# A new order of all engines' work in a Mamba-2 scan with a low-rank mixer, and V loaded in one transfer

## The chip, the core and the metric

The kernel runs on one core of a Trainium2 chip. Its engines work at the same time, each through its own list of instructions in a fixed order: TensorE (PE, matrix products; its weight loads are shown as PEld), VectorE (DVE), ScalarE (ACT), GpSimd (POOL) and SyncE (SP), whose queue issues all transfers here. They meet through semaphores: an instruction that waits holds up all that stand behind it on its engine. The metric is the device time of one execution in microseconds (us).

## The reference

Four batches, 8 heads, 768 positions. First a Mamba-2 scan in chunks of 32 positions with head width 32 and state width 16, then a mixer over positions of rank 32 and a two-layer network over the 256 channels:

```python
# scan, per chunk of 32
cum = np.cumsum(log_a, -1);  M = (C @ B.T) * exp(cum_i - cum_j) * causal
y = M @ x + (C @ state) * exp(cum)
state = exp(sum(log_a)) * state + sum_j B_j x_j exp(cum_end - cum_j)
# mixer, x is y as (batch, seq, 256)
h = (x.transpose(0, 2, 1) @ U) @ V
u = x + h.transpose(0, 2, 1)
out = u + np.maximum(u @ w_ch1, 0.0) @ w_ch2
```

x, a, B and C are 32-bit. U, V, w_ch1 and w_ch2 arrive as 64-bit numbers and are made 32-bit on the chip from their two words.

## The kernel before, in words

A batch of 768 positions is cut into three pairs of blocks of 128, so there are 12 pairs. The core does for each pair the scan, and for each batch the mixer (`project`, `mixed`, `added`) and then, in three blocks of 256 positions, the network. The order of everything is written out by hand in `PLANS`: strings of words, read by `follow` from left to right. A word calls one step, which emits its instructions, and each engine runs the instructions it gets in the order of the words. So two steps on different engines may overlap, and two on the same engine never change places.

The number behind a letter of the scan is the pair, counted from the first pair of batch 1: -3, -2 and -1 are batch 0, 0 to 2 are batch 1, and so on. The words that matter here:

- B and X load a pair's B, C (three transfers) and x (two). w0 to w8 load parts of the weights, L is a later pair's B and X together. Words B, X, w and L are held: their first transfer waits until the last DVE instruction emitted ahead of the word is done (`until`, `hold`).
- A and K make the decay factors from a (`decays`, `keep`). F puts that many filler products ahead of the next bank that is taken.
- P or Q multiplies B and C with decays (DVE; Q does a quarter or a half: 0 and 1 are B's two blocks, 2 is C). T or V turns the result on PE, and ACT or DVE copies it out. D or E multiplies B with the decay to the chunk's end (POOL in batch 0, DVE later).
- g makes C times B (PE, four banks), m and M mask its halves (two DVE instructions each), s makes the states' increments (PE), u carries the state on (DVE, then POOL or ACT).
- n and i add the two parts of y (PE), j is the second half of i and begins with a small copy on DVE that waits for the products before it when nothing else does. y copies the result (ACT), t or O turns it to rows per position and copies it (ACT, for O-1.1 DVE).
- c0 is the conversion of U and V, c1 and c2 of w0 and w1, c3 of w2, and so on. A c word is one of three steps: DVE and ACT, ACT, then DVE (`to_fp32`). v spreads V over the partitions (`spread`). R splits a weight into a near and a far part (`refine`): ACT first, the second R word with DVE.
- p, x, a are project, mixed and added of a mixer, S splits a block. The first number of these words is how many batches the mixer lies behind batch 1: 1 is batch 0, 0 is batch 1. U1.j.i is a quarter i of the hidden layer of block j of batch 0 in 32-bit products (`plain`). It needs `added` of its half of the positions: block 0 needs a1.0, block 1 needs both a1.0 and a1.1. For the other blocks f, e and h are its first products, second products and the two DVE steps behind them (`first`, `second`, `third`). d is a piece of the second layer (`down`).

The PSUM banks on which PE writes are 2 of tag w, 3 of x and 3 of z. A step that needs a bank waits until the readers of an older one are done.

V has 32 rows of 768 numbers. `Vq` holds it as 128 rows of 192: before, rows 32q to 32q+31 are its q-th quarter of columns. `spread` makes of it `V4`, in which each group of 32 partitions holds the rows of V with one half of its columns, by eight products with pieces of the identity.

Of the kernel before, what the change touches and what calls it, by code (L numbers as in the profile page):

```python
# [33 lines left out]

PLANS = {
    0: (
        'B0 X0 B1 X1 B2 X2 V0 U0 B3 '),
    1: (
        'w0 F5 A0 w1 Q-3.0 Q-3.1 B4 A1 w2 Q-3.2 F4 V-3.0.0 V-3.1.1 Q-2.2 B5 X3 Q-2.0 Q-2.1 K0 '
        'D-3 w3 w4 g-3 m-3 D-2 V-2.0.2 s-3 u-3 F2 V-2.1.2 M-3 Q-1.1 n-3 s-2 X4 Q-1.0 g-2 u-2 '  # L40
        'Q-1.2 V-1.0.2 m-2 M-2 w5 F1 V-1.1.3 i-3 c0 B6 c0 E-1.0 E-1.1 F1 s-1 u-1 c0 g-1 w6 w7 '
        'j-3 y-3 n-2 i-2 j-2 y-2 P0 c1 c1 m-1 M-1 T0 t-2 T0 n-1 c1 i-1 c2 c2 v0 j-1 y-1 P1 T1 '
        'O-3.0 T1 g0 c2 c3 m0 M0 O-1.1 p1 g1 D1 D0 s0 c3 X5 P2 m1 M1 x1 a1.0 u0 U1.0.0 T2 T2 '
        'a1.1 c5 U1.1.0 c3 s1 c4 c5 c5 n0 R0 i0 y0 c4 U1.0.1 U1.1.1 R1 w8 c4 X6 L4 P3 D2 c6 c6 '
        'R2 g2 c7 c7 U1.1.2 U1.1.3 t0 u1 T3 T3 U1.0.2 m2 M2 c7 i1 c6 n1 L5 L6 c8 c8 y1 c9 c9 '
        'U1.0.3 d1.0 c8 d1.1 n2 R5 s2 R4 c9 d1.0 d1.1 S1.2 u2 i2 P4 y2 R1 R0 T4 t1 d1.1 D4 R4 '
        'f1.2.1 R5 R3 f1.2.0 P5 T4 D3 R7 R3 R2 R7 d1.0 d1.0 e1.2.0 e1.2.1 h1.2.0 d1.1 h1.2.1 '
        'f1.2.2 f1.2.3 R6 t2 e1.2.2 g4 m4 M4 p0 h1.2.2 g3 m3 e1.2.3 M3 T5 d1.0 T5 R6 d1.2 L7 '
        'd1.2 x0 s3 a0.0 h1.2.3 d1.2 d1.2 S0.0 d1.2 d1.2 d1.2 d1.2 a0.1 u3 f0.0.1 f0.0.0 P6 P7 '
        'f0.0.2 d1.2 d1.2 d1.2 d1.2 e0.0.0 e0.0.1 e0.0.2 d1.2 d1.1 f0.0.3 n3 s4 i3 y3 h0.0.0 '  # L50
        'e0.0.3 T6 T6 h0.0.1 u4 h0.0.2 g5 m5 M5 h0.0.3 d0.0 d0.0 d0.0 d0.0 D5 d0.0 i4 D6 n4 S0.1 '
        'y4 s5 u5 d0.0 f0.1.3 d0.0 d0.0 i5 n5 y5 s6 u6 f0.1.2 f0.1.0 d0.0 d0.0 S0.2 e0.1.2 '
        'h0.1.2 L8 e0.1.0 f0.1.1 d0.0 d0.0 T7 e0.1.1 h0.1.1 f0.2.2 e0.1.3 f0.2.0 e0.2.2 h0.1.3 '
        'h0.2.2 f0.2.1 e0.2.0 h0.1.0 d0.1 d0.1 d0.1 h0.2.0 t5 f0.2.3 e0.2.1 P8 d0.1 d0.1 d0.1 '
        'e0.2.3 h0.2.3 h0.2.1 D7 d0.1 d0.2 d0.2 d0.1 d0.2 d0.2 t3 T7 d0.1 d0.1 d0.2 d0.1 d0.1 '
        'd0.0 T8 T8 D8 d0.2 d0.2 d0.2 t4 g7 m7 M7 p-1 g6 m6 M6 s7 d0.2 d0.2 d0.2 u7 d0.2 x-1 '
        'a-1.0 a-1.1 d0.1 d0.2 S-1.0 i6 n6 s8 y6 i7 S-1.1 n7 y7 u8 f-1.0.1 g8 m8 M8 f-1.0.0 '
        'f-1.0.2 f-1.0.3 e-1.0.0 e-1.0.1 h-1.0.0 h-1.0.1 f-1.1.1 S-1.2 f-1.1.0 f-1.1.2 e-1.0.2 '
        'h-1.0.2 e-1.0.3 t6 e-1.1.0 f-1.1.3 e-1.1.2 h-1.1.2 d-1.0 d-1.0 d-1.0 h-1.1.0 d-1.0 '
        'f-1.2.2 e-1.1.3 f-1.2.0 e-1.1.1 d-1.0 h-1.0.3 d-1.0 d-1.0 h-1.1.1 e-1.2.2 h-1.2.2 '  # L60
        'e-1.2.0 d-1.1 d-1.0 d-1.1 h-1.1.3 h-1.2.0 d-1.1 d-1.1 d-1.1 d-1.1 t7 d-1.1 d-1.1 i8 n8 '
        'd-1.1 d-1.1 d-1.1 y8 t8 p-2 d-1.1 x-2 a-2.0 S-2.0 d-1.0 f-1.2.3 f-1.2.1 d-1.0 d-1.0 '
        'd-1.0 e-1.2.3 e-1.2.1 h-1.2.3 f-2.0.0 a-2.1 d-1.2 h-1.2.1 f-2.0.1 d-1.2 d-1.2 d-1.2 '
        'S-2.1 d-1.2 e-2.0.0 h-2.0.0 d-1.2 d-1.2 f-2.0.3 f-2.0.2 S-2.2 d-1.2 f-2.1.2 e-2.0.1 '
        'h-2.0.1 e-2.0.2 e-2.0.3 h-2.0.2 d-1.2 d-1.2 e-2.1.2 d-1.2 d-1.2 f-2.1.3 f-2.1.0 h-2.1.2 '
        'f-2.1.1 f-2.2.2 e-2.1.0 e-2.1.1 d-2.0 d-2.0 d-2.0 d-2.0 e-2.2.2 h-2.0.3 d-2.0 d-2.0 '
        'f-2.2.0 e-2.1.3 d-2.0 d-2.0 f-2.2.3 d-2.2 f-2.2.1 h-2.1.0 h-2.1.3 e-2.2.3 d-2.0 d-2.1 '
        'd-2.1 d-2.1 d-1.1 h-2.1.1 e-2.2.0 d-2.1 h-2.2.3 d-2.1 d-2.1 d-2.1 h-2.2.0 d-2.1 e-2.2.1 '
        'h-2.2.1 d-2.0 d-1.2 d-2.0 d-2.0 d-2.2 d-2.1 h-2.2.2 d-2.1 d-2.1 d-2.1 d-2.0 d-2.2 d-1.0 '
        'd-2.2 d-2.2 d-2.2 d-2.1 d-2.2 d-2.2 d-2.2 d-2.2 d-2.2 d-2.2 d-2.2 '),  # L70
}


# [1 line left out]
def kernel(  # L75
# [43 lines left out]
    Q = 32  # L119
# [38 lines left out]
    class Kept:  # L158
# [6 lines left out]
        def __getattr__(self, name):  # L165
# [23 lines left out]
    def hold(load, until):  # L189

        tc.add_manual_dep(load.ins, until.ins.name, mybir.DependencyInfo(
            mybir.DependencyClass.Sync, mybir.DependencyReason.DATA))

    def begin(**kwargs):
        op = nc.sync.dma_start(**kwargs)  # L195
        if until:
            hold(op, until.pop())
# [24 lines left out]
    UV = const.tile([P, 2, NC * RK], FP32)  # L222
    U_sb = UV[:, 0].rearrange("p (c r) -> p c r", c=NC)
    Vq = UV[:, 1]
    V4 = const.tile([P, VS], FP32)
    w1 = [const.tile([P, NCB, DF], FP32R, name=f"w1{i}") for i in range(3)]
    w1all = const.tile([P, NQ, NCB, W], FP32, name="w1f")
    w1f = [w1all[:, c] for c in range(NQ)]
    w2 = [const.tile([P, NM, DM], FP32R, name=f"w2{i}") for i in range(3)]
    weights = []  # L230

    def words_of(dst):
        p, i, j = dst.shape
        t = raw.tile([P, 2 * WCOLS], INT32, tag="words", name="words", bufs=NWORDS)
        weights.append((dst, t[:p, :2 * i * j]))
        return t[:p, :2 * i * j]

    def each(parts, *index):
        return [part[index] for part in parts]

    def load_words(dst, src):

        p, i, j = dst.shape
        t = words_of(dst)
        begin(out=t.rearrange("p (i j) -> p i j", i=i), in_=src)

    U2, V2, w12, w22 = (w.bitcast(INT32) for w in (moe_U, moe_V, moe_w_ch1, moe_w_ch2))
    every = slice(None)
    quarter = WCOLS // NCB
    w13 = w12.rearrange("(c p) m -> p c m", p=P)  # L250
    own = {}

    def load_v():
        own["UV"] = words_of(UV)
        for q in range(4):
            begin(out=own["UV"][ts(q, Q), 2 * NC * RK:], in_=V2[:, ts(q, 2 * NC * RK)])

    def load_u():
        begin(out=own["UV"][:, :2 * NC * RK].rearrange("p (c r) -> p c r", c=NC),
                          in_=U2.rearrange("(c p) r -> p c r", p=P))  # L260

    def load_w(n):
        if n < 2:
            if n == 0:
                own["w"] = words_of(w1f[0])
                weights.pop()
            dst, t = w1f[0][:, :, ts(n, P)], own["w"][:, ts(n, 2 * NCB * P)]
            weights.append((dst, t))
            begin(out=t.rearrange("p (i j) -> p i j", i=NCB),
                  in_=w13[:, :, ts(n, 2 * P)])  # L270
        elif n <= NQ:
            load_words(w1f[n - 1], w13[:, :, ts(n - 1, 2 * quarter)])
        else:
            m = 2 * (n - NQ - 1)
            load_words(w2[0][:, m:m + 2], w22[m * P:(m + 2) * P].rearrange(
                "(m p) d -> p m d", p=P))

    def load(k):
        if k < NB * NPR:
            load_bc(k)  # L280
            load_x(k)

# [45 lines left out]
    for g in range(2):  # L328
# [3 lines left out]
        out=la.rearrange("p b c h -> p b h c"),  # L332
# [180 lines left out]
    def turn(*args):  # L513
        for _ in turning(*args):
            pass
# [414 lines left out]
    def spread():  # L930

        v = [bank(t, VS // 2) for t in "xz"]
        for q in range(4):
            for i in range(2):
                rows = ts(2 * (q % 2) + i, Q)
                nc.tensor.matmul(out=v[i][ts(q, Q)], lhsT=ident[rows, rows], rhs=Vq[rows],
                                 start=True, stop=True, skip_group_check=True)
        for i in range(2):
            nc.scalar.copy(out=V4[:, ts(i, VS // 2)], in_=v[i])

# [22 lines left out]
    def ytokens_of(k, v):  # L963
# [3 lines left out]
                 M=lambda k: mask(k, (2, 3)), u=update, i=lambda k: inter(k, 0), n=intra,  # L967
                 j=crossed, y=yout, t=ytokens, L=load, Q=lambda k, c: prep(k, c, 1),
                 E=lambda k, c: decayed(k, c, 1), O=ytokens_of,
                 V=lambda k, c, v: turn(k, c, 1, "wx"[v // 2], vector if v % 2 else None))  # L970
    whole = dict(c=convert, R=refined, A=lambda i: decays(every_batch, "w", [i]),
                 K=lambda n: keep(every_batch, "z"), F=fill,
                 v=lambda n: spread())
# [54 lines left out]
```

## Time and profile before

| what | value |
|---|---|
| median of 3 runs | 226.31 us (225.0 to 226.91) |
| profiled execution, its own time | 225.08 us |
| span from its first to its last instruction | 223.4 us |
| mean granted clock of TensorE | 0.977 of full speed |
| PE busy | 213.6 us (96%), 3374 products |
| DVE busy | 164.5 us (74%) |
| ACT busy | 129.0 us (58%) |
| POOL busy | 6.6 us (3%) |
| bytes moved | 14.61 MB, mean 65 GB/s |

In the page's second part the span is cut in 40 slices of about 5.6 us; each digit is a busy share in tenths, PEclk the clock that TensorE was granted in tenths of full speed. In the view by stretches a line gives the stretch, its length, then busy us and number of instructions of PE, PEld, DVE, ACT and POOL, then the granted clock, the share of the transfer engines and GB/s. In the order of time a line gives start, duration, engine, line of the source, operation, operands and count, and in brackets how long the engine had been idle and what released it. All DVE work is emitted on line 169, a helper, so it is told apart by its tiles.

### The profile page before, as it was taken

Reading aid. Unit: us, or ns where it says so; the run is one execution under the profiler, and the core shown is the slowest. Engines: PE = TensorE matmul, PEld = TensorE weight load, DVE = VectorE, ACT = ScalarE, POOL = GpSimd, SP = SyncE. Lnnn points to the kernel's source line nnn. Section 1 sums busy time; section 2 is a strip of 40 time slices with the busy share of each in tenths; the row PEclk is TensorE's granted clock in tenths of the full one; section 3 lists DMA queues with packets and bytes.
Section 4 is the critical chain, followed back from the end, with each engine's and each line's share of the span. In section 5 each row is a group of like instructions: output and inputs, shape, how many; then the busy total and the mean of one; then the engine's idle time right before and its main releaser. Section 6 shows DMA issues by size and latency. Waiting matters only on the chain.

```text
span 223.4 us, 7740 instructions
## 1 busy us (share of the span) xinstructions
PE 213.6 (96%) x3374; PEld 191.7 (86%) x3374; DVE 164.5 (74%) x341; ACT 129.0 (58%) x293; POOL 6.6 (3%) x22
## 2 busy tenths in 40 slices
PE   7867899999999999999999999999999999999994
PEld 5646675878889988989999997799998999999994
DVE  3588789989989989789279748849882694917641
ACT  2334492999749755587875361878433447545430
POOL 4213000000000000000000000000000000000000
PEclk9996599999999999999999999999999999999999
DMA  5987999898680005023016010200000000000132
GB/s 85 132 111 135 195 154 254 171 247 121 82 118 7 1 3 94 3 39 109 3 13 84 3 47 3 100 3 1 3 0 3 3 1 0 3 0 0 56 135 94
DMA packets 69345, 14.61 MB, mean 65 GB/s; under 512 B 63616, under 2 KB 67520, under 8 KB 69312
## 3 DMA queue, kind: packets, MB, share of 16 engines
q1 hardware_dynamic: 69312, 14.13, 33.0%
q8 instruction: 26, 0.43, 0.9%
q14 instruction: 7, 0.06, 0.1%
HBM read 10.98 MB, written 3.15 MB: 63 GB/s over the span
## 4 chain that ended last, share of the span: by engine, by line
PE 84%; DVE 4%; SPq 4%; ACT 4%; DMA 2%; issue 1%; DVEq 0%; ACTq 0%
PE x L784 34%; PE z L784 26%; SPq L195 4%; PE x L529 2%; PE w L742 2%; PE w L713 2%; DMA bc<-in_B_dram 2%; PE w L903 2%; PE x L684 2%; PE z L684 2%; PE x L659 2%; PE w L497 2%; PE z L659 1%; DVE M L169 1%; PE w L564 1%; PE x L753 1%
## 5 line engine op out<-in xcount | busy, mean ns | idle before, releaser
L169 DVE SCALAR_TENSOR_TENSOR words<-words 128x512 fp32r<-128x512 f32 (+6 forms) x60 | 39.7, 673 | 9.2 <-PE x L784 4.3
L784 PE MATMUL x<-words,w 128*128 128x256 f32 x288 | 39.0, 281 | 0.0
L784 PEld LDWEIGHTS x<-words,w 128*128 128x128 f32 x288 | 35.4, 188 | 1.0 <-issue 0.5
L784 PE MATMUL z<-u,w 128*128 128x256 f32 x240 | 34.4, 282 | 0.0
L784 PE MATMUL x<-u,w 128*128 128x256 f32 x240 | 33.6, 282 | 0.0
L784 PEld LDWEIGHTS z<-u,w 128*128 128x128 f32 x240 | 30.4, 189 | 0.5 <-issue 0.2
L784 PEld LDWEIGHTS x<-u,w 128*128 128x128 f32 x240 | 30.1, 188 | 0.4 <-issue 0.2
L789 ACT ACTIVATE z<-z 128x512 f32<-128x512 f32 (+1 forms) x24 | 13.8, 573 | 14.8 <-PE z L784 14.6
L789 ACT ACTIVATE x<-x 128x512 f32<-128x512 f32 (+1 forms) x27 | 15.2, 571 | 9.4 <-PE x L784 7.3
L784 PE MATMUL z<-words,w 128*128 128x256 f32 x144 | 19.2, 280 | 0.0
L784 PEld LDWEIGHTS z<-words,w 128*128 128x128 f32 x144 | 17.5, 188 | 0.3 <-issue 0.2
L169 DVE SCALAR_TENSOR_TENSOR words<-x,words 128x512 fp32r<-128x512 f32 x20 | 13.7, 686 | 4.6 <-ACT words L824 4.6
L169 DVE SCALAR_TENSOR_TENSOR words<-z,words 128x512 fp32r<-128x512 f32 x20 | 13.7, 685 | 2.8 <-ACT words L824 2.8
L824 ACT ACTIVATE words<-x 128x512 fp32r<-128x512 f32 x20 | 11.9, 599 | 6.3 <-PE x L784 6.3
L824 ACT ACTIVATE words<-z 128x512 fp32r<-128x512 f32 x20 | 11.8, 597 | 5.0 <-PE z L784 4.9
L596 ACT ACTIVATE Sm<-S,slot 128x128 f32<-128x128 f32 (+1 forms) x18 | 6.1, 389 | 12.3 <-DVE S L169 12.3
L169 DVE SCALAR_TENSOR_TENSOR S<-S,kept,w 128x64 f32<-128x64 f32 x40 | 11.2, 280 | 2.1 <-PE w L564 0.4
L169 DVE TENSOR_TENSOR BC<-bc,F 128x512 f32<-128x512 f32 (+2 forms) x18 | 9.5, 548 | 3.2 <-ACT F L372 1.5
L169 DVE TENSOR_TENSOR u<-yT,u 128x512 fp32r<-128x512 f32 x10 | 6.9, 690 | 6.5 <-ACT u L778 6.5
L169 DVE TENSOR_TENSOR yT<-x,yT 128x384 f32<-128x384 f32 (+1 forms) x15 | 9.2, 615 | 2.2 <-ACT x L789 1.0
L529 PE MATMUL z<-Cm,T 32*64 32x128 f32 x192 | 10.6, 317 | 0.0
L529 PE MATMUL x<-Cm,T 32*64 32x128 f32 x192 | 10.6, 317 | 0.0
(148 smaller groups left out, 391.5 us busy)
## 6 DMA issues: line engine op xcount, KB each, us to landing
words<-in_moe_w_ch_dram SPq DMA_DIRECT2D x7, 512.0 KB, 5.7
x<-in_x_dram SPq DMA_DIRECT2D x24, 128.0 KB, 3.7
out_dram<-o SPq DMA_DIRECT2D x8, 256.0 KB, 2.2
bc<-in_B_dram SPq DMA_DIRECT2D x24, 64.0 KB, 3.6
bc<-in_C_dram SPq DMA_DIRECT2D x12, 128.0 KB, 4.0
out_dram<-words SPq DMA_DIRECT2D x3, 256.0 KB, 2.6
words<-in_moe_w_ch_dram SPq DMA_DIRECT2D x2, 256.0 KB, 3.5
out_dram<-o SPq DMA_DIRECT2D x2, 128.0 KB, 1.7
```

Source lines behind the costliest of these rows:

```text
L169: self.last = call(*args, **kwargs)
L195: op = nc.sync.dma_start(**kwargs)
L497: nc.tensor.transpose(out=tp[:, i, v], in_=s["BC"][:, i, c + v].rearrange("p h n -> p (h n)"), identity=ident)
L529: nc.tensor.matmul(out=g[r][cols, c], lhsT=s["T"][rows, 0, c, cols], rhs=s["Cm"][rows, :, :, ts(2 * c + p, Q)].rearrange("r v t i -> r v i ...
L596: nc.scalar.activation(s["Sm"][:, sl, v], s["S"][:, sl, ts(v, D)], AF.Copy, scale=slot[:, v, None])
L659: product = nc.tensor.matmul(out=y[r // 2][p][ts(v, H), c], lhsT=own[ts(r, Q)], rhs=s["T"][ts(r, Q), 1, :, ts(2 * c + p, Q)].rearrange("r ...
L684: product = nc.tensor.matmul(out=y[n][p][ts(v, Q), c], lhsT=x_sb[k][half, c, h], rhs=s["M"][half, h // 2, c, h % 2], start=fresh(k, n, p, ...
L713: nc.tensor.transpose(out=t[:, c, g], in_=yT[b][:, g, ts(2 * q + c, P)], identity=ident)
L742: nc.tensor.matmul(out=p[ts(q, Q)], lhsT=U_sb[:, c], rhs=ytok[b][:, c, ts(q // 2, P)], start=(c == 0), stop=(c == NC - 1), skip_group_chec ...
L784: nc.tensor.matmul(out=t, lhsT=lhsT, rhs=rhs, start=start, stop=True, skip_group_check=True)
L789: nc.scalar.activation(t, t, AF.Copy, scale=1.0 + EPS)
L824: nc.scalar.activation(gs[j, i][0], t, AF.Relu, scale=NEAR)
```

## The change

The plan has the same words as before except for U and V, so the same steps, in another order. Word V (four transfers of 32 partitions) and word U become Z1 and Z0 of a step `load_uv`, which has no hold. V comes in one transfer of 128 partitions, in which four partitions hold the four quarters of one row of V, and `spread` takes the columns of the identity that fit. The list of weights becomes a dictionary with the same numbers. The first plan loses V0, U0 and B3; Z1, Z0 and B3 stand in the second. The parts of the plan that are spoken of below:

```diff
     0: (
-        'B0 X0 B1 X1 B2 X2 V0 U0 B3 '),
+        'B0 X0 B1 X1 B2 X2 '),
     1: (
-        'w0 F5 A0 w1 Q-3.0 Q-3.1 B4 A1 w2 Q-3.2 F4 V-3.0.0 V-3.1.1 Q-2.2 B5 X3 Q-2.0 Q-2.1 K0 '
-        'D-3 w3 w4 g-3 m-3 D-2 V-2.0.2 s-3 u-3 F2 V-2.1.2 M-3 Q-1.1 n-3 s-2 X4 Q-1.0 g-2 u-2 '
-        'Q-1.2 V-1.0.2 m-2 M-2 w5 F1 V-1.1.3 i-3 c0 B6 c0 E-1.0 E-1.1 F1 s-1 u-1 c0 g-1 w6 w7 '
-        'j-3 y-3 n-2 i-2 j-2 y-2 P0 c1 c1 m-1 M-1 T0 t-2 T0 n-1 c1 i-1 c2 c2 v0 j-1 y-1 P1 T1 '
-        'O-3.0 T1 g0 c2 c3 m0 M0 O-1.1 p1 g1 D1 D0 s0 c3 X5 P2 m1 M1 x1 a1.0 u0 U1.0.0 T2 T2 '
-        'a1.1 c5 U1.1.0 c3 s1 c4 c5 c5 n0 R0 i0 y0 c4 U1.0.1 U1.1.1 R1 w8 c4 X6 L4 P3 D2 c6 c6 '
...
-        'd1.2 x0 s3 a0.0 h1.2.3 d1.2 d1.2 S0.0 d1.2 d1.2 d1.2 d1.2 a0.1 u3 f0.0.1 f0.0.0 P6 P7 '
-        'f0.0.2 d1.2 d1.2 d1.2 d1.2 e0.0.0 e0.0.1 e0.0.2 d1.2 d1.1 f0.0.3 n3 s4 i3 y3 h0.0.0 '
...
+        'F5 A0 Q-2.0 Q-3.0 Q-3.1 A1 Q-3.2 F4 V-3.0.0 V-3.1.1 Q-2.2 K0 g-3 m-3 V-2.0.2 Q-1.0 D-2 '
+        'D-3 s-3 Q-2.1 F2 V-2.1.2 Q-1.2 V-1.0.2 M-3 n-3 Q-1.1 F1 V-1.1.3 Z1 Z0 u-3 w0 w1 g-2 B3 '
+        's-2 u-2 i-3 j-3 y-3 m-2 E-1.1 c0 c0 E-1.0 M-2 c0 g-1 i-2 w2 F1 s-1 n-2 u-1 B4 j-2 m-1 '
+        'c2 c2 y-2 M-1 O-3.0 c1 i-1 j-1 P0 c2 B5 X3 w3 c3 c1 c1 P1 t-2 w4 w5 X4 T0 T0 c3 n-1 y-1 '
+        'v0 T1 c3 T1 w6 O-1.1 P2 g0 m0 R0 w7 D0 p1 T2 B6 T2 M0 x1 s0 a1.0 a1.1 c4 X5 c4 c4 g1 D1 '
+        'U1.1.0 U1.1.1 w8 m1 c5 u0 c5 X6 L4 L5 L6 M1 U1.0.0 U1.0.1 D2 i0 c5 n0 y0 s1 c7 u1 c6 g2 '
...
+        'd1.2 a0.0 d1.1 a0.1 D4 S0.0 d1.2 d1.2 g4 s3 d1.2 d1.2 d1.2 f0.0.0 m4 u3 d1.2 D5 f0.0.1 '
+        'L7 e0.0.0 f0.0.2 e0.0.1 M4 f0.0.3 h0.0.0 e0.0.2 s4 n3 h0.0.1 i3 e0.0.3 d1.0 d1.2 u4 '
...
-    def load_v():
-        own["UV"] = words_of(UV)
-        for q in range(4):
-            begin(out=own["UV"][ts(q, Q), 2 * NC * RK:], in_=V2[:, ts(q, 2 * NC * RK)])
-
-    def load_u():
-        begin(out=own["UV"][:, :2 * NC * RK].rearrange("p (c r) -> p c r", c=NC),
-                          in_=U2.rearrange("(c p) r -> p c r", p=P))
+    def load_uv(n):
+        if "UV" not in own:
+            own["UV"] = words_of(0, UV)
+        if n:
+            begin(out=own["UV"][:, 2 * NC * RK:], in_=V2.rearrange("r (q c) -> (r q) c", q=4))
+        else:
+            begin(out=own["UV"][:, :2 * NC * RK].rearrange("p (c r) -> p c r", c=NC),
+                  in_=U2.rearrange("(c p) r -> p c r", p=P))
...
-                rows = ts(2 * (q % 2) + i, Q)
-                nc.tensor.matmul(out=v[i][ts(q, Q)], lhsT=ident[rows, rows], rhs=Vq[rows],
-                                 start=True, stop=True, skip_group_check=True)
+                nc.tensor.matmul(out=v[i][ts(q, Q)],
+                                 lhsT=ident.rearrange("p (r q) -> p q r", q=4)[:, 2 * (q % 2) + i],
+                                 rhs=Vq, start=True, stop=True, skip_group_check=True)
```

## The prediction

> **What bounds the kernel now.** I read the page first, for where TensorE (PE) stands idle.
>
> ```profile
> PE   7867899999999999999999999999999999999994
> ...
> DVE  3588789989989989789279748849882694917641
> ...
> PEclk9996599999999999999999999999999999999999
> ```
>
> PE has no free tenth after the eighth slice, and its clock is low in the fourth and fifth. The view of busy time by stretches, cut where the clock changes and where the dense work begins, makes this sharp:
>
> ```profile
> 11.95:15.36 3.41, 2.24 (x100) 1.66 (x100) 2.53 (x10) 1.93 (x7) 0.61 (x1) 1.00 0.89 107
> 15.36:18.77 3.41, 1.93 (x62) 1.25 (x44) 3.17 (x11) 0.53 (x3) 1.45 (x3) 1.00 0.64 130
> 18.77:22.19 3.42, 3.42 (x83) 2.75 (x82) 2.41 (x9) 1.80 (x5) 0.34 (x1) 0.50 0.80 131
> ```
>
> ```profile
> 36.10:217.00 180.90, 180.43 (x2649) 166.47 (x2646) 137.88 (x260) 111.06 (x246) 0.00 (x0) 1.00 0.24 48
> ```
>
> From 36.1 to 217 us PE idles 0.47 us in all. No order of the same work can gain more than that there, but one can lose. So what can be won lies before 36 us, and I ask when the dense work can start. VectorE (DVE) is the one to follow there; its order of time has these lines:
>
> ```profile
> 6.41 0.94 DVE L169 TENSOR_TENSOR BC<-bc,F 128x128 f32<-128x128 f32 x3 [1.52 <-ACT F L372]
> ...
> 9.63 1.52 DVE L169 TENSOR_TENSOR BC<-bc,F 128x256 f32<-128x256 f32 x3 [0.98 <-DMA bc<-in_C_dram]
> ...
> 15.33 0.49 DVE L169 TENSOR_TENSOR BC<-bc,F 128x128 f32<-128x128 f32 x2 [0.67 <-DMA bc<-in_B_dram]
> ...
> 20.32 0.63 DVE L169 TENSOR_SCALAR words<-words 128x384 int32<-128x384 int32 x2 [0.87 <-DMA words<-in_moe_U_dram]
> ...
> 24.81 0.15 DVE L169 COPY settled<-slot 128x1 f32<-128x1 f32 x1 [1.19 <-PE z L659]
> ```
>
> ```profile
> 15.33:34.53 19.20, 16.45 (x443) 12.11 (x426) 15.69 (x48) 10.37 (x27) 2.20 (x4) 0.73 0.85 161
> ```
>
> DVE waits for data at 9.63, 15.33 and 20.32 us. From 15.33 to 34.53, when it has made the last token copies of batch 0 (O-1.1), it works 15.69 of 19.20 us: 3.51 us idle. Last the queue of SP, and PE where the dense work begins:
>
> ```profile
> 4.96 0.58 SPq L195 DMA_DIRECT2D bc<-in_B_dram  x1
> ...
> 13.13 3.14 SPq L195 DMA_DIRECT2D words<-in_moe_V_dram  x4
> 16.32 0.43 SPq L195 DMA_DIRECT2D words<-in_moe_U_dram  x1
> ```
>
> ```profile
> 37.77 1.99 PE L784 MATMUL x<-yT,w1f 128*128 128x256 f32 x8
> 39.60 0.60 PE L497 MATMUL w<-ident,BC 128*128 128x128 f32 x4
> 40.04 1.89 PE L784 MATMUL x<-yT,w1f 128*128 128x256 f32 x8
> ```
>
> The first of these is U1.0.0 (to 39.60: 1.83 us), the last U1.1.0.
>
> **Loads and spread.** V in one transfer takes three issues from SP. The four took 3.14 us; one costs from 0.43 (U's) to 0.92 us (x's second load before it), I take U's, the nearest in size. U then goes out near 13.6 instead of 16.32, and lands after its 3.88 us (20.20 less 16.32) near 17.5. Its reader c0 comes on DVE at 20.8 (below), so the 0.87 us wait is gone and 3.3 us of cover are left; were U later than that, c0 would wait by the excess. The eight products of `spread` now take all 128 rows: 16 passes lasted from 29.50 to 30.05. As a price from above I take the pT products (128 rows to 32 columns, 48 in 1.08 + 0.76 us, 38 ns for 128 columns, 57 for 192): 0.92 us, so between 0 and +0.37, nearer the upper end by shape. They lie beside c3 on DVE, which decides when x1 can run, so nothing is added; uncovered it is 0.37. The Trainium skill, "TensorE: Matmul & The Clock Gate", Part 3, says that K=32 products in different row groups run at once; by that rule the two groups used become serial, which would double 0.55 us. The trace does show two groups starting 10 ns apart.
>
> **Holds on SP.** Z words have no hold. w0, w1 and B3 now wait for u-3, w2 for the end of c0, B4 for u-1, B5, X3 and w3 for the end of c2. SP so stands from about 14 to 18 us, where before it never paused ahead of 33 us. B5 is then issued from 30.8, 31.9 for its last; with 3.4 us to land (as the first pairs) that is 35.3, against its reader P2 at 35.7. Latencies reach 5.2 where the queue is full: up to +1.4 us. I take 0 and keep 1.4.
>
> **The early order.** Up to X2 the SP queue is the same, so landings are too. DVE now begins with Q-2.0, whose block of B is issued at 4.96 and needs 3.4 us: 8.38. Q-3.0 to Q-3.2, which ran at 6.41, queue behind it: 9.60 instead of 7.35 at the end, +2.25. K0 and V-3 move with it; m-3 starts at 12.74 instead of 12.07, since the wait for C (9.61) falls away. Behind it Q-1.0, Q-2.1, Q-1.2 and M-3 end at 14.97, and Q-1.1 waits for the same landing as before (15.31). So the loss is swallowed, and what is left is that at 15.33 u-3 (1.19 us) is not done, while Q-1.0 and Q-1.2 (0.27 + 0.34) are. D-3 now follows D-2 on POOL (0.69 each), so s-3 is at 13.1 instead of 11.4; u-3 comes after 16.9 anyhow.
>
> **DVE work from 15.33 to the end of O-1.1.** 15.69 before; plus u-3 1.19; plus the last step of c3 1.98 (1.29 + 0.69), now ahead of O-1.1; less the 0.61; less m0 and M0 (1.34), now behind it: 16.91 us.
>
> **Its waits**, by the order on PE and ACT: V-1.1.3 needs the bank that ACT frees after V-2.1's copies: 15.6 to 16.5, 0.9. u-2 needs s-2 behind g-2, whose bank V-1.1.3 holds until 17.35: 18.1 to 18.75, 0.65. u-1 needs s-1, now behind g-1, i-2 and a fill, with g-1 waiting until 21.7 for z banks that y-3 and M-2 free: 23.8 to 24.85 at half clock, 1.05. The small copies ahead of j-2 and j-1 wait for n-2 and i-1: 0.55 and 0.35. Sum 3.5 us, as much as before (3.51) in other places. From below it is 0; from above I allow 6, as if each wait were as long as the 1.19 above.
>
> **Start of U.** Behind O-1.1 DVE has P2 0.61, m0 and M0 1.34, D0 0.34, and, as U1.1.0 is now the first product, both a1.0 and a1.1 (0.94 each): 4.17 us. So U1.1.0 starts at 15.33 + 16.91 + 3.5 + 4.17 = 39.9 us. x1, s0 and g1 (1.65 + 0.45 + 0.8 us) fill PE meanwhile. Before, U1.1.0 started at 40.04 with U1.0.0 already done; all other PE work ahead of it is the same. So PE is late by 39.9 + 1.83 - 40.04 = 1.7 us. Past this point PE has at most 0.47 us to give back. c4 to c9 have their weights in time by the same queue (w3 lands near 39, c4 at 40.2).
>
> The profiled execution took 225.08 us (223.4 of span and 1.7 around it), which gives 226.8. It lies 1.23 us under the median of the runs, 226.31; against that the forecast is 228.0.
>
> **The rivals.** *Slower in the dense part.* A first and second product (f, e) of a hidden quarter are 12 products of 0.117 us, 1.41; the two DVE steps that free their bank (h) take 1.37. A stretch such as "f0.0.0 m4 u3 d1.2 D5 f0.0.1 L7 e0.0.0 f0.0.2 e0.0.1 M4", where before P6, P7 and four d stood ahead of e0.0.0, puts 2.9 us of other DVE work (u3, m4, M4, D5) among them with few d to cover it. For it: DVE is busy in nine tenths of many dense slices. Against: before has the like and idles 0.47. Each such place missed costs 0.7 to 1.4 us; two or three on top of the forecast give 229.5 to 231.
>
> *Not slower: the waits close up.* The waits on DVE between 15.33 and 36 us are the whole loss. If its idle time falls under 1.8 us (3.5 less 1.7), the same order is faster; with none it gives 1.8 us, 224.5, and with the last 0.47 regained 224.1. For it: the data waits (0.87) are gone and DVE's order is denser. Against: four of my five waits follow from banks and products in order.
>
> *Clock stays full.* The clock fell at 18.77 after a stretch with PE busy 1.93 of 3.41 us, and held through 2.24. My order makes about 2.2 there, a toss. At full clock g-1, i-2, the fill and n-2 are 1.5 us shorter and two waits go: 226.5. The Trainium skill (same page, Part 1) has the clock fall after an idle window of about 3.4 us. The trace disagrees: PE's longest wait there was 1.48 us. By the rule it would not fall now, with 2.1 us as the longest wait, and the time would be this one.
>
> *No doing of it:* the loads do land earlier, but only 0.87 us hung on them; V alone would give under that.
>
> **How the numbers follow.** Forecast (waits of 2.5 to 5 us, 227 to 229.5): 0.42. Clock full: 0.13. Waits close up: 0.18. Dense stalls: 0.27. Within 1% (about what a measurement of this kernel can tell from no change) means 224.05 to 228.57. Of the forecast 0.22 lies inside and 0.20 above; clock full lies inside; of closed waits 0.05 lies inside and 0.13 under it, as my sum may err by 1 us; dense stalls lie above. Faster 0.13, same 0.40, slower 0.47. The range, leaving a tenth at each side: 224.3 to 230.8, from closed waits to three dense stalls.
>
> **What would show it.** The first DVE preparation at 8.4, not 6.4; c0 without a wait for U; u-1 waiting for s-1 and a low clock from 18.8; U1.1.0 at about 39.9; PE without idle after that. U before 38.2 would make the walk wrong; idle time of over 1 us between 42 and 217 would make the dense part the cause.

## The result, and the profile after

| what | before | after |
|---|---|---|
| median, 22 executions each | 225.49 us (223.95 to 226.98) | 226.81 us (225.25 to 228.36) |
| profiled execution, its own time | 225.08 us | 227.02 us |
| its span | 223.4 us | 225.3 us |
| its mean granted clock | 0.977 | 0.968 |

The ratio is 1.0059, 95% interval 1.0037 to 1.0081: 1.3 us slower, by this interval more than nothing and under 1%. The forecast was 228.0 us, with 224.3 to 230.8 as its range. In the experiments below the median is that of all executions, while ratio and interval leave out those in the chip's slower state (three with V alone, one with the late new order, four with the first fillers).

The page of the changed kernel, its second part:

```profile
span 225.3 us, 7753 instructions
...
PE   7887999899999999999999999999999999999994
...
DVE  3378798798989899896957947959883779545541
...
PEclk9997559999999999999999999999999999999999
```

Behind the fourth slice and ahead of the last, PE has one digit under 9, an 8 in the eighth (39.4 to 45.1 us), where the dense work begins; the low clock now reaches into the sixth slice. By stretches (length, busy us and number of PE, PEld, DVE, ACT, POOL, granted clock, transfer share, GB/s):

```profile
11.95:15.36 3.41, 2.95 (x111) 1.86 (x104) 2.87 (x9) 2.32 (x9) 0.57 (x1) 1.00 0.93 123
15.36:18.77 3.41, 2.50 (x97) 1.56 (x77) 1.71 (x7) 0.77 (x3) 0.61 (x1) 1.00 0.49 121
...
22.19:32.40 10.21, 9.69 (x261) 7.85 (x249) 8.48 (x26) 5.41 (x13) 0.51 (x1) 0.50 0.68 111
...
42.00:217.00 175.00, 173.78 (x2611) 160.96 (x2610) 134.07 (x252) 107.94 (x240) 0.00 (x0) 1.00 0.24 47
```

In the second row DVE does 1.71 us of work, where before it did 3.17 in the same 3.41 us at the same full clock. In the last, PE idles 1.22 us. DVE in order of time says where both come from:

```profile
8.26 1.03 DVE L169 TENSOR_TENSOR BC<-bc,F 128x128 f32<-128x128 f32 x4 [3.33 <-DMA bc<-in_B_dram]
...
16.27 0.61 DVE L169 TENSOR_SCALAR Cm<-x,slot 128x128 f32<-128x128 f32 x2 [0.98 <-PE x L496]
...
18.64 1.30 DVE L169 SCALAR_TENSOR_TENSOR S<-S,kept,w 128x64 f32<-128x64 f32 x4 [0.60 <-PE w L563]
...
20.58 0.82 DVE L169 TENSOR_SCALAR words<-words 128x384 int32<-128x384 int32 x2
...
24.81 0.91 DVE L169 SCALAR_TENSOR_TENSOR S<-S,kept,w 128x64 f32<-128x64 f32 x3 [1.17 <-PE w L563]
...
34.77 0.76 DVE L169 COPY ytok<-z 128x256 f32<-128x256 f32 x2 [0.16 <-PE z L712]
...
41.39 0.76 DVE L169 TENSOR_SCALAR words<-words 128x512 int32<-128x512 int32 x2 [1.06 <-DMA words<-in_moe_w_ch_dram]
...
44.53 0.75 DVE L169 TENSOR_TENSOR M<-x,causal 128x256 int32<-128x256 int32 x2
```

These are Q-2.0, V-1.1.3, u-2, c0 (no wait for U any more), u-1, O-1.1, c4 (which waits for its weights) and m1. PE at the start of the dense work, U1.1.0, its sister and U1.0.0:

```profile
40.16 1.99 PE L783 MATMUL x<-yT,w1f 128*128 128x256 f32 x8
41.99 1.89 PE L783 MATMUL z<-yT,w1f 128*128 128x256 f32 x8
45.01 1.99 PE L783 MATMUL x<-yT,w1f 128*128 128x256 f32 x8 [1.12 <-DVE M L169]
```

U1.0.0 needs the bank that m1 reads, and m1 stands behind c4. The queue of SP gives c4's reason; the second line follows the first stand, w3 is the first of the three in the third:

```profile
14.06 0.43 SPq L195 DMA_DIRECT2D words<-in_moe_U_dram  x1
18.06 2.21 SPq L195 DMA_DIRECT2D words<-in_moe_w_ch_dram  x2
...
34.33 2.00 SPq L195 DMA_DIRECT2D words<-in_moe_w_ch_dram  x3
```

Where the time went: the words x0, x-1 and x-2, deep in the dense part, start at 85.11, 138.47 and 172.53 us before and at 87.52, 141.14 and 175.23 after. PE is 2.4 us late at the first and 2.7 at the last, so 2.4 is made before 85 us and next to nothing later. Behind x-2 it wins 0.97 back (last section) and ends 1.74 late. The word x1, ahead of U, starts at 36.12 before and at 37.43 after: 1.3 of the 2.4 us are there already at x1.

### The profile page after: what moved, and what is told of

Read it like the earlier page. It is cut to its first block, busy times and chain, and to the rows that moved or that the text cites. A ratio compares the mean times of both kernels' runs of the same rounds, so it can differ in the third digit from the quotient of the medians.

```text
span 225.3 us, 7753 instructions
## 1 busy us (share of the span) xinstructions
PE 215.7 (96%) x3374; PEld 193.0 (86%) x3374; DVE 164.4 (73%) x342; ACT 129.4 (57%) x293; POOL 6.5 (3%) x22
## 5 line engine op out<-in xcount | busy, mean ns | idle before, releaser
L169 DVE SCALAR_TENSOR_TENSOR words<-words 128x512 fp32r<-128x512 f32 (+6 forms) x60 | 39.4, 668 | 3.1 <-PE x L783 0.8
L783 PE MATMUL x<-words,w 128*128 128x256 f32 x288 | 39.8, 283 | 0.0
L783 PEld LDWEIGHTS x<-words,w 128*128 128x128 f32 x288 | 35.5, 188 | 1.6 <-issue 1.3
L783 PE MATMUL z<-u,w 128*128 128x256 f32 x240 | 33.1, 280 | 0.0
L783 PEld LDWEIGHTS z<-u,w 128*128 128x128 f32 x240 | 29.9, 188 | 0.4 <-ACT yT L702 0.3
L169 DVE SCALAR_TENSOR_TENSOR words<-x,words 128x512 fp32r<-128x512 f32 x20 | 13.7, 687 | 12.6 <-ACT words L823 12.5
L783 PE MATMUL z<-words,w 128*128 128x256 f32 x144 | 19.8, 281 | 0.0
L169 DVE SCALAR_TENSOR_TENSOR words<-z,words 128x512 fp32r<-128x512 f32 x20 | 13.7, 685 | 2.6 <-ACT words L823 2.6
L528 PE MATMUL x<-Cm,T 32*64 32x128 f32 x192 | 11.7, 318 | 0.8 <-ACT T L509 0.8
L169 DVE TENSOR_TENSOR BC<-bc,F 128x512 f32<-128x512 f32 (+2 forms) x18 | 8.8, 507 | 3.9 <-DMA bc<-in_B_dram 3.3
L169 DVE TENSOR_TENSOR yT<-z,yT 128x384 f32<-128x384 f32 (+1 forms) x12 | 7.1, 595 | 6.0 <-PE z L783 6.0
L658 PE MATMUL z<-T,Sm 32*64 32x64 f32 x180 | 8.9, 257 | 1.5 <-DVE settled L169 1.3
```

The costliest lines, as they stand in the source:

```text
L169: self.last = call(*args, **kwargs)
L528: nc.tensor.matmul(out=g[r][cols, c], lhsT=s["T"][rows, 0, c, cols], rhs=s["Cm"][rows, :, :, ts(2 * c + p, Q)].rearrange("r v t i -> r v i ...
L658: product = nc.tensor.matmul(out=y[r // 2][p][ts(v, H), c], lhsT=own[ts(r, Q)], rhs=s["T"][ts(r, Q), 1, :, ts(2 * c + p, Q)].rearrange("r ...
L783: nc.tensor.matmul(out=t, lhsT=lhsT, rhs=rhs, start=start, stop=True, skip_group_check=True)
```

## The experiments

In each diff of the plan a line of "..." stands for words that are the same. The time at half clock of an execution is 2 × (1 − mean granted clock) × span; it differs between executions of one kernel (the last section), so I use it to compare kernels.

**Two theories first.** A: the places of the loads and their holds are the loss. B: the order of the first 60 us is. One rival, the dense part. The one part that stands by itself, V, comes first, on before's order:

```diff
-        'B0 X0 B1 X1 B2 X2 V0 U0 B3 '),
+        'B0 X0 B1 X1 B2 X2 Z1 Z0 B3 '),
```

> The order of before, word for word, with Z1 and Z0 in the places of V0 and U0: only the one transfer of V and the spread with 128 rows are new. My theory (the loads alone give under 0.87 us, because DVE next waits for PE at 24.81): SP takes about 0.5 us for V instead of 3.14, U lands near 17.5, DVE does not wait for U; time 0 to 0.9 us less than before, U1.0.0 at 37.0 to 37.8. Rival (the loads are what costs: more traffic from one row's four parts, or the spread on 128 rows in the way): 0.4 us or more over before.

225.84 us, ratio 1.0039 (0.9984 to 1.0094): no gain, a small loss not excluded. U's reader still waits:

```profile
20.29 0.63 DVE L169 TENSOR_SCALAR words<-words 128x384 int32<-128x384 int32 x2 [0.72 <-DMA words<-in_moe_U_dram]
```

U was issued at 14.93 instead of 16.32, and came 5.3 us later instead of 3.9. In this execution the load's earlier issue was worth 0.15 us. U1.0.0 came at 38.96, not at 37.0 to 37.8 as expected; this execution had 13.65 us at half clock where the first of before had 10.24.

The loads and holds, put back into the new order:

```diff
-        'B0 X0 B1 X1 B2 X2 '),
+        'B0 X0 B1 X1 B2 X2 Z1 Z0 B3 '),
...
-        'F5 A0 Q-2.0 Q-3.0 Q-3.1 A1 Q-3.2 F4 V-3.0.0 V-3.1.1 Q-2.2 K0 g-3 m-3 V-2.0.2 '
+        'w0 F5 A0 w1 Q-2.0 Q-3.0 B4 Q-3.1 w2 A1 Q-3.2 F4 V-3.0.0 V-3.1.1 B5 X3 Q-2.2 K0 g-3 m-3 w3 w4 V-2.0.2 '
...
```

> The new order of all computing words, with the words of the loads put back to the places that they have in before (so w0 to w7 and B3 to B6 are issued early, and SP does not stand from 14 to 18 us). Theory A (the holds make w3 late, so c4, m1 behind it on DVE and then U1.0.0 on PE are late): c4 does not wait for w3, the 1.1 us wait of PE at 43.5 shrinks to 0.3 or less, time 1.0 to 1.5 us under the changed kernel. Theory B (the early order of the engines is the cost, the holds are harmless): time within 0.5 us of the changed kernel, U1.1.0 again near 40.

226.91 us, ratio 1.0079 (1.0035 to 1.0123). Its profile shows what A wants: c4 without a wait, PE without one near 43.5.

```profile
38.85 0.75 DVE L169 TENSOR_SCALAR words<-words 128x512 int32<-128x512 int32 x2
```

But the time is that of the changed kernel. A is not the loss alone. One caution for what follows: the profiled execution is among the three fastest of the ten (225.27 us), with x1 at 36.04 and x0 at 85.01, as before (36.12 and 85.11). So this profile does not show the loss that the median has.

The order, cut at S1.2 (near 67 us): before's words up to there with Z1 and Z0, and behind it the words that are left, in the new order; the diff shows its first lines. Then the reverse.

```diff
-        'B0 X0 B1 X1 B2 X2 '),
+        'B0 X0 B1 X1 B2 X2 Z1 Z0 B3 '),
-        'F5 A0 Q-2.0 Q-3.0 Q-3.1 A1 Q-3.2 F4 V-3.0.0 V-3.1.1 Q-2.2 K0 g-3 m-3 V-2.0.2 Q-1.0 D-2 '
+        'w0 F5 A0 w1 Q-3.0 Q-3.1 B4 A1 w2 Q-3.2 F4 V-3.0.0 V-3.1.1 Q-2.2 B5 X3 Q-2.0 Q-2.1 K0 '
...
```

> The order of before up to S1.2 (the end of the first U stage), the new order behind it, V in one transfer. My theory (all that is lost is lost before 46 us): within 0.9 us of before, on the lower side, mixer 0's x at about 85.1, no PE wait over 0.5 us behind 60 us. Rival (new stalls in the dense part): 0.7 us or more over before, with PE waits behind 60 us.

226.65 us, ratio 1.0090 (1.0053 to 1.0128). It says less than hoped, as the seam costs by itself; of the 1.8 us by which x0 is late here (86.90), this wait is 1.3:

```profile
68.85 0.97 PE L783 MATMUL x<-u,w 128*128 128x256 f32 x6 [1.30 <-ACT w L450]
```

> The new order up to S1.2, the order of before behind it. My theory: as the changed kernel, 1.0 to 2.7 us over before, U1.1.0 near 40.2 and a PE wait near 43.5 again. Rival (the dense part is the cost): within 0.5 us of before.

227.44 us, ratio 1.0138 (1.0058 to 1.0219; four executions), with pauses of PE of 0.58 us ahead of 112.34 and 0.61 ahead of 144.80. The first neither kernel has; ahead of 142.7 before has one of 0.38 and 0.49 in its two profiles. The profile names nothing that PE waited for there, and the wait near 43.5 that I expected did not come. So these two say little on where the loss lies: a cut and joined order has losses of its own. Both kernels once more, beside the later experiments:

> The kernel before once more, for a second profile. If the stretch of half clock and the two rates of the network's products (113.3 and 117.8 ns from start to start) belong to the order of the work, they stand where they stood (half clock from 18.8 to 29.0 us, 117.8 ns from 168 to 203 us). If they hang on the moment at which an execution begins, they stand elsewhere, and the start of U1.0.0 (37.77) moves by half a us or more with the half clock.

> The changed kernel once more, for a second profile. The DMA landing at 8.26 that the first DVE work waits for, and U1.1.0 as the first product, come again by either theory. If U1.1.0's start (40.16) belongs to the order, it is within 0.4 us of that; if the half clock (13.7 us of it in the first profile, 10.2 in the profile of before) set it, it moves with the length of the half clock. PE waits near 43.5 again if w3's late issue is the cause.

224.0 and 226.7 us. In the second PE does not wait for m1: a1.1 ends 1 us later there, c4 comes right behind it at 41.35, and U1.1.0 at 41.28. From 42 to 217 us PE idles 0.09 us there, where the first profile has 1.22. The 1.12 us of the first profile and the later start are the same loss in two shapes, not to be added: U1.0.0 starts at 45.01 and 44.96. The waits of DVE differ too between the two profiles of the changed kernel, that of u-2 most, 0.60 and 1.52 us:

```profile
19.25 1.30 DVE L169 SCALAR_TENSOR_TENSOR S<-S,kept,w 128x64 f32<-128x64 f32 x4 [1.52 <-PE w L563]
```

**New theory: what the new order puts ahead of U** (c3's last step, both halves of a1). It is the prediction's own account. On the kernel with the loads back:

```diff
-        'v0 T1 c3 T1 O-1.1 P2 g0 m0 R0 D0 p1 T2 X5 T2 M0 x1 s0 a1.0 a1.1 c4 c4 c4 '
+        'v0 T1 T1 O-1.1 P2 g0 m0 R0 D0 p1 T2 X5 T2 M0 x1 s0 a1.0 U1.0.0 a1.1 c3 c4 c4 c4 '
...
```

> The kernel with the new order and the loads in the places of before, and two words moved: the last step of c3 from ahead of O-1.1 to behind a1.1, and U1.0.0 to between a1.0 and a1.1 (so that it is the first product, as before). My theory (these 1.98 us of c3 and 0.94 of a1.1 ahead of the first product are most of the loss): the first product of U starts 2 to 2.5 us earlier than without the two moves (38.77), at 36.2 to 36.8 us, and the time is 1 to 2.5 us under the changed kernel's, at or under before. Rival (the early waits are the loss): first product at 38 us or later, time not under the changed kernel's by more than 0.5 us.

227.53 us, ratio 1.0085 (1.0052 to 1.0119). DVE, nearly two microseconds lighter, stands instead, for PE at half clock (until 33.09):

```profile
34.33 0.76 DVE L169 COPY ytok<-z 128x256 f32<-128x256 f32 x2 [2.07 <-PE z L712]
```

The first product of U comes at 38.82, not at 36.2 to 36.8 as I had put down. The theory falls: what was taken from ahead of O-1.1 on DVE became a wait for PE in this execution, and the time did not fall.

**The clock.** Fillers in two thin places, on before's order with Z1 and Z0, then on the changed kernel:

```diff
-        'n-3 s-2 X4 '
+        'n-3 F3 s-2 X4 '
...
-        'E-1.0 E-1.1 F1 s-1 u-1 '
+        'E-1.0 E-1.1 F3 s-1 u-1 '
```

> The order of before with V in one transfer, and two words added to: F3 ahead of s-2 and F3 in place of F1 ahead of s-1, so PE makes 3 and 2 more filler products in the stretch where the clock fell. If the low clock costs time before U starts: the clock stays full through 18.8 to 29 us or is low for under 4 us, x1 starts 1 to 2 us earlier (34.1 to 35.1 with the first profile of before as measure) and the time falls by 0.7 to 2 us against before. If DVE and the landings set the pace there: x1 within 0.5 us of 36.1, time within 0.5 us of before or above it by the fillers' 1 us.

226.03 us, ratio 1.0012 (0.9973 to 1.0052). The time did not fall by the 0.7 to 2 us expected. In the profiled execution the clock stays full, and x1 comes 1.2 us earlier than before (34.96), but PE then pauses 1.44 us in the middle of i0, and the span is 224.2:

```profile
43.75 0.35 PE L658 MATMUL z<-T,Sm 32*64 32x64 f32 x3 [1.44 <-issue]
```

What it waited for is not shown: "issue" means that the profile has nothing, and the state that these products read (Sm) had been written on ACT by 38.85.

```diff
-        'B3 s-2 u-2 '
+        'B3 F3 s-2 u-2 '
...
-        'w2 F1 s-1 n-2 u-1 '
+        'w2 F4 s-1 n-2 u-1 '
```

> The changed kernel with three filler products ahead of s-2 and three more ahead of s-1; no other step moves. If the longer stretch at half clock (13.65 us, against 10.24 before) makes up most of the loss, the clock stays full in most executions, O-1.1 ends 1 to 1.5 us earlier than 35.5, U1.1.0 starts near 38.9 instead of 40.16, and the median falls to the kernel before or under it: ratio 0.995 to 1.001. If the loss lies in the order, the ratio stays at 1.004 to 1.008 even in the executions at a mean clock of 0.99 and above, and where the clock falls all the same, the six fillers cost 0.2 to 1.4 us more.

227.76 us, ratio 1.0109 (1.0061 to 1.0157), with 3.4 us at half clock where the changed kernel's profile has 13.7. The fillers lie on the path of u-2 and u-1, which wait for products that queue behind them:

```profile
19.48 1.30 DVE L169 SCALAR_TENSOR_TENSOR S<-S,kept,w 128x64 f32<-128x64 f32 x4 [1.75 <-PE w L563]
...
26.62 0.91 DVE L169 SCALAR_TENSOR_TENSOR S<-S,kept,w 128x64 f32<-128x64 f32 x3 [2.19 <-PE w L563]
```

0.60 and 1.17 us have become 1.75 and 2.19: 2.2 us given for the clock, or 1.2 against the second profile of the changed kernel (1.52 and 1.22). So this could not give the clock's share. All executions together can. Over 81 executions of before (those beside the experiments) and the 22 of after, one slope and one offset fitted: 0.12 us (standard error 0.015) for each us at half clock, and after 1.4 us (0.17) later at an equal time at half clock. The 81 come in four sets, each beside other experiments; with one set at a time the offset is 0.9 to 1.6, so it is less sure than its standard error says. After's mean time at half clock is 12.2 us against 10.0, which makes 0.3. By this fit the clock is about a fifth of the loss, and the order the rest.

**Two places of the order, alone.** m1 ahead of c4:

```diff
-        's0 a1.0 a1.1 c4 X5 c4 c4 g1 D1 U1.1.0 U1.1.1 w8 m1 c5 '
+        's0 a1.0 a1.1 g1 m1 D1 c4 X5 c4 c4 U1.1.0 U1.1.1 w8 c5 '
```

> The changed kernel with g1, m1 and D1 ahead of the first c4 instead of behind the last. If m1 behind the wait of c4 for w3 is a loss of its own, m1 comes near 41 instead of 44.5, TensorE's wait of 1.1 us near 43.5 is gone, U1.0.0 starts near 43.9 instead of 45.0 and the end comes 0.5 to 1.1 us earlier: ratio 1.001 to 1.004. If the wait only moves (c4 and u0 are then late, and U1.0.0 or i0 waits for them), a like wait shows within 5 us behind it and the ratio stays near 1.006.

226.02 us, ratio 1.0037 (1.0004 to 1.0069); at equal half clock 0.9 us (0.2) over all executions of before, 0.5 (0.2) over those beside it. DVE and the dense rows of this kernel:

```profile
41.21 0.76 DVE L169 TENSOR_TENSOR M<-x,causal 128x256 int32<-128x256 int32 x2
41.88 0.41 DVE L169 TENSOR_TENSOR bd<-bc,FD 128x256 f32<-128x256 f32 x1
42.22 0.76 DVE L169 TENSOR_SCALAR words<-words 128x512 int32<-128x512 int32 x2
```

```profile
42.00:217.00 175.00, 174.76 (x2620) 162.23 (x2619) 133.84 (x251) 108.26 (x240) 0.00 (x0) 1.00 0.24 48
```

m1 comes at 41.21 instead of 44.53, and x0 starts 0.44 us earlier (87.08). PE's idle time is 0.24 us instead of 1.22, but the move need not be why: the second profile of the changed kernel has 0.09 without it. U1.0.0 comes at 44.68, 0.3 us earlier than in either of these. The middle of the ratio lies between the two expectations; part of the loss at most.

Then the early order, mended at single words:

```diff
-        'F5 A0 Q-2.0 Q-3.0 Q-3.1 A1 Q-3.2 F4 V-3.0.0 V-3.1.1 Q-2.2 K0 g-3 m-3 V-2.0.2 Q-1.0 D-2 '
-        'D-3 s-3 Q-2.1 F2 V-2.1.2 Q-1.2 V-1.0.2 M-3 n-3 Q-1.1 F1 V-1.1.3 Z1 Z0 u-3 w0 w1 g-2 B3 '
+        'F5 A0 Q-3.0 Q-3.1 A1 Q-3.2 F4 V-3.0.0 V-3.1.1 Q-2.2 Q-2.0 K0 g-3 m-3 V-2.0.2 Q-1.0 D-3 '
+        'D-2 s-3 Q-2.1 F2 V-2.1.2 Q-1.2 V-1.0.2 M-3 n-3 u-3 Q-1.1 F1 V-1.1.3 Z1 Z0 w0 w1 g-2 B3 '
...
-        'M-2 c0 g-1 i-2 w2 F1 s-1 n-2 u-1 B4 '
+        'M-2 c0 s-1 g-1 u-1 i-2 w2 F1 n-2 B4 '
```

> The changed kernel with the early order of before's kind: Q-2.0 back behind V-3.1.1, D-3 ahead of D-2, u-3 ahead of Q-1.1, s-1 ahead of g-1 and u-1 ahead of i-2. If the waits of VectorE between 15 and 25 us are the loss (0.98, 0.60 and 1.17 us), their sum falls from 2.75 to under 1.5 us, O-1.1 ends at 34.0 to 34.8 instead of 35.5, U1.1.0 starts near 39 and the ratio falls to 1.000 to 1.003. If TensorE at half clock sets the same pace (as with U1.0.0 moved ahead, where VectorE waited 2.07 us ahead of O-1.1), a new wait stands ahead of j-1 or O-1.1, O-1.1 ends within 0.4 us of 35.5, and the ratio stays at 1.004 to 1.008.

226.84 us, ratio 1.0048 (1.0022 to 1.0075). It didn't do what it was to do: U1.1.0 comes at 41.19, not near 39. The wait of u-1 is gone, but that of u-2 has grown to 2.32 us,

```profile
19.77 1.30 DVE L169 SCALAR_TENSOR_TENSOR S<-S,kept,w 128x64 f32<-128x64 f32 x4 [2.32 <-PE w L563]
```

because s-2 still stands on PE behind V-1.0.2, V-1.1.3 and g-2; before it stands ahead of them. The next diff undoes that too.

**All suspects at once.** Before's order and places of loads up to u-1, with Z1 and Z0; behind it the new order, c3 and a1 ahead of U as there, with m1 ahead of c4:

```diff
-        'B0 X0 B1 X1 B2 X2 '),
+        'B0 X0 B1 X1 B2 X2 Z1 Z0 B3 '),
...
-        'F5 A0 Q-2.0 Q-3.0 Q-3.1 A1 Q-3.2 F4 V-3.0.0 V-3.1.1 Q-2.2 K0 g-3 m-3 V-2.0.2 Q-1.0 D-2 '
-        'D-3 s-3 Q-2.1 F2 V-2.1.2 Q-1.2 V-1.0.2 M-3 n-3 Q-1.1 F1 V-1.1.3 Z1 Z0 u-3 w0 w1 g-2 B3 '
-        's-2 u-2 i-3 j-3 y-3 m-2 E-1.1 c0 c0 E-1.0 M-2 c0 g-1 i-2 w2 F1 s-1 n-2 u-1 B4 j-2 m-1 '
+        'w0 F5 A0 w1 Q-3.0 Q-3.1 B4 A1 w2 Q-3.2 F4 V-3.0.0 V-3.1.1 Q-2.2 B5 X3 Q-2.0 Q-2.1 K0 '
+        'D-3 w3 w4 g-3 m-3 D-2 V-2.0.2 s-3 u-3 F2 V-2.1.2 M-3 Q-1.1 n-3 s-2 X4 Q-1.0 g-2 u-2 '
+        'Q-1.2 V-1.0.2 m-2 M-2 w5 F1 V-1.1.3 i-3 c0 B6 c0 E-1.0 E-1.1 F1 s-1 u-1 j-3 y-3 c0 g-1 '
...
-        's0 a1.0 a1.1 c4 X5 c4 c4 g1 D1 U1.1.0 U1.1.1 w8 m1 '
+        's0 a1.0 a1.1 g1 m1 D1 c4 X5 c4 c4 U1.1.0 U1.1.1 w8 '
```

> Three suspects undone at once: before's order, with before's places for the loads of weights, up to u-1 (V0 and U0 replaced by Z1 and Z0), then the rest in the changed kernel's order, with g1, m1 and D1 ahead of the first c4. At an equal time at half clock the changed kernel took 1.1 us more than before, with m1 alone moved 0.7, with the early repairs alone 0.8, with the loads alone back 1.3. If these three hold the loss between them, little is left: TensorE starts U1.1.0 at 38.5 to 39.5 us, x0 at 85 to 86, and the ratio is 0.998 to 1.002. If the loss lies in what stands between u-1 and U1.1.0 (c3's last step and both halves of a1 ahead of U), or behind it, U1.1.0 starts near 40 or later for the same time at half clock, and the ratio stays at 1.004 to 1.008.

224.77 us, ratio 0.9997 (0.9968 to 1.0026): the loss is gone. At equal half clock it lies 0.3 us (0.2) under all executions of before, 0.1 (0.3) under those beside it, and 1.7 (0.2) under after. (By this fit the four figures of the expectation, 1.1, 0.7, 0.8 and 1.3 us, are each 0.2 to 0.3 larger; their order is the same.) Behind u-1 every word but g1, m1 and D1 stands in the changed kernel's order, loads aside. So neither the new dense part nor c3 and a1 ahead of U cost anything that can be seen here. Its stretches and DVE's lines for c0, O-1.1 and a1.0:

```profile
15.36:18.77 3.41, 2.14 (x72) 1.46 (x59) 3.10 (x12) 0.69 (x3) 1.44 (x3) 1.00 0.99 183
...
42.00:217.00 175.00, 174.99 (x2627) 162.78 (x2627) 133.15 (x249) 107.96 (x240) 0.00 (x0) 1.00 0.21 42
```

```profile
19.21 0.63 DVE L169 TENSOR_SCALAR words<-words 128x384 int32<-128x384 int32 x2
...
32.82 0.75 DVE L169 COPY ytok<-z 128x256 f32<-128x256 f32 x2
...
37.77 0.56 DVE L169 TENSOR_TENSOR yT<-x,yT 128x384 f32<-128x384 f32 x1 [1.94 <-PE z L752]
```

In the first row DVE works 3.10 us again from 15.36 to 18.77. This row parts the kernels by their early order, whatever else they have. With before's early order it is 3.17, 3.10 (before again), 2.76 (V alone), 3.03 (new from S1.2) and 3.10, or 2.38 with fillers; with the new one 1.71, 1.59 (after again), 1.94 (loads back), 1.58 (before's from S1.2), 2.00 (c3 behind), 1.58 (fillers), 1.58 (m1 early) and 1.49 (single words mended). Wherever the loads stand, DVE has some 1.3 us less done here with the new early order (3.0 against 1.7 on average, without the row of fillers on before's order): it waits for V-1.1.3's bank and for s-2. The row is a mark of the order and not the size of its cost: the profile with the loads back has 1.94 in it and is not late at x0.

Up to O-1.1 the whole stretch can be compared, first of the changed kernel, then of this one, each from Q-1.1 on:

```profile
15.01:34.77 19.76, 17.44 (x445) 13.12 (x430) 15.90 (x48) 10.10 (x26) 2.77 (x5) 0.65 0.64 120
```

```profile
15.15:32.82 17.67, 12.39 (x398) 9.09 (x392) 15.71 (x44) 9.85 (x27) 2.20 (x4) 0.99 0.86 165
```

DVE's work is nearly the same, 15.90 and 15.71 us, and its idle time falls from 3.86 to 1.96. A part of this is the clock, 0.65 of full speed against 0.99. O-1.1 comes 1.95 us earlier than in the changed kernel, x0 1.99 (85.53), x-2 2.40 (172.83), the last product 2.14 (219.95). This profile has only 3.4 us at half clock, so by the fit some 1.2 of these are the clock's; the timed comparison, with 11.3 us there on average, is not touched by that. U1.1.0 does not gain all that O-1.1 does: a1.0 now waits 1.94 us for PE, and U1.1.0 comes at 39.56 instead of 40.16, U1.0.0 at 43.12 instead of 45.01.

How the loss divides among the early order, the loads' places and m1 stays open. Against the changed kernel at equal half clock the loads alone gave nothing measurable (0.25 us slower, standard error 0.25), m1 alone about 0.4 us (0.2), the early order mended at single words 0.3 (0.2), and all together 1.7. The early order alone was never undone whole with the new places of the loads.

## Why the prediction came out as it did

**The place: right.** "What can be won lies before 36 us": the lag is made before x0, and the rival of dense stalls fell. By the prediction's own sign (PE idle over 1 us between 42 and 217) the first profile, with 1.22, would speak for that rival. But 1.12 of it is the wait at 45.01, at the start of U, the second profile has 0.09, and the last experiment keeps the new dense order without a loss.

**The walk of DVE: right, as a sum against before.** Work to the end of O-1.1 was put at 16.91 us and is 16.61 in the 20.48 us from 15.01 to 35.49; waits at 3.5 and are 3.87; the end at 35.74 and is about 35.5. The three larger waits came at 0.98, 0.60 and 1.17 against 0.9, 0.65 and 1.05; of the two small ones (0.55 and 0.35) one came, at 0.38. U1.1.0 came at 40.16 against 39.9 (41.28 when run again), PE's lag behind it is 40.16 + 1.83 − 40.04 = 1.95 against 1.7, and the profiled executions differ by 1.94. The closeness is in part luck. Work was put 0.3 too high and waits 0.4 too low; the second profile has 1.52 instead of 0.60 at u-2. The sum has no wait for m1, which in the first profile raised PE's lag to 2.4 us at x0, and it was the 0.97 won behind x-2, at the products' faster rate, that brought the difference at the end back to 1.9.

**What the sum was read to mean: half wrong.** I took the waits as neutral ("as much as before, in other places") and the loss as work, c3's last step and a second half of a1 ahead of U. Moving just these gained nothing; leaving them there and undoing the early order, with the loads and m1, gained all, and DVE's idle time up to O-1.1 fell by 1.9 us at nearly the same work. So the step that failed is the reading of the waits as no part of the loss; how much of it is theirs, and how much the loads' and m1's, stays open. A sum against before can come out right while another term is the one to change.

**"A loss swallowed" by the landing at 15.31: wrong.** Q-1.1 did not even wait for it (15.01). Right behind, from 15.36 to 18.77, DVE does 1.46 us less than before. How much of the time that costs is not shown by itself.

**"c4 to c9 have their weights in time": wrong.** w3 was put at 39. It was issued from 34.33, and the page's median for these transfers in the changed kernel is 7.0 us; c4 waits 1.06 us to 41.39. The cover was thought to be 1.2 us, and the price with the cover gone is m1 behind c4: about 0.4 us of the time, by the experiment with m1 alone.

**Loads: right in the main.** U out at 14.06 (13.6 was said) and landed at 18.52 (17.5), c0 without a wait, the SP queue standing from 14.5 to 18.06 (14 to 18), P2 without a wait for B5. That V alone gives under 0.87 us: it gave none that could be measured.

**Spread.** At full clock (with fillers) the 16 passes take 0.91 us, from 27.95 to 28.86: the 0.92 taken from the pT row, not 0.55. In the changed kernel they ran at half clock and took 1.5. The Trainium skill, "TensorE: Matmul & The Clock Gate", Part 3, would have doubled 0.55 to 1.10; the direction agrees, the row was the better measure of the size.

**Clock.** "A toss", with about 2.2 us of PE work in the stretch that decides: that stretch had 1.78 (1.88 when run again), and the clock fell. It was down for 13.4 us or more in 15 of 22 executions, before in 35 of 81. The forecast, built on the 10.2 of before's profile, did not hold this; 0.3 us by the fit. By the rule of the Trainium skill, Part 1 of the same page (the clock falls after an idle window), it would have stayed up. The runs speak against that, as the trace of before did (last section).

**Base.** 228.0 was anchored to 226.31, the median of three. That of 22 executions is 225.49, and 0.8 of the 1.2 us by which the forecast is too high is this anchor. Slower by more than 1% was given 0.47 and a time within 1% 0.40; it came out within 1%.

## What to carry to other kernels

An equal sum of waits before and after does not clear the waits: they can still be what there is to win, so price what the order would take without them. Before charging work as late, look whether the engine at its other end, at the clock it has there, would be any earlier. Where an order is undone word by word with little to show, undo one whole stretch with its loads: here the single repairs gave 0.4, 0.3 and nothing, the whole 1.7 us. And profile a kernel more than once before one wait in it is called its cost: m1's 1.12 us stood in one profile of the changed kernel and not in the other.

## What the runs showed of the hardware

**The granted clock has a step and a phase of its own.** It changes only at marks 3.41 us apart, and these marks lie elsewhere in each execution (the first at 4.6 to 7.9 us). So one kernel spends 0 to 17 us at half clock: before takes 224.2 us (median of 8) without a step and 225.7 (30) with four. In 14 profiles it fell 14 times (twice in one, in one not) in the first 33 us, each time behind a stretch of 3.41 us in which PE was busy 1.11 to 2.76 us, and never behind an empty one. There it fell behind each stretch with less than 2.05 us, and with 2.05 to 2.76 it went both ways. At the end of two executions (V alone and before again) it held behind 1.71 and 1.92, so PE's busy time alone does not settle it. The Trainium skill, "TensorE: Matmul & The Clock Gate", Part 1, has a free-running window of about 3.4 us, which agrees with the marks. Its rule that the clock falls after an idle window does not fit these falls, none of which had one ahead of it.

**Two rates of the same product.** The network's products of 128 columns by 256 follow one another at 113.3 or at 117.8 ns, at one for some ten to thirty us. Before ran its last dense stretch (from about 170 to 203 us) at 117.8, after ran at 113.3 there; the 0.97 us won behind x-2 goes with that. The share of slow products is 0.50 and 0.22 in two executions of before, 0.38 and 0.32 of after. So it changes between executions of one kernel; whether the order has a part in it, and what sets it, is not known.

**One issue has no fixed price.** V's single transfer held SP 0.58 us in the changed kernel and 1.77 in the last experiment, where the four of before held it 3.14 and 1.98. So a count of issues times the cheapest row, as in the prediction, is a lower bound.
